# Nyström attention feeding a mixture of experts: batch 0's hidden layer split by token half, one pseudo-inverse chain for batches 2 and 3, and a new order

## The chip, the cores and the metric

The kernel runs on one core of one Trainium2 chip. The metric is the device time of one execution in microseconds. Three runs of the kernel before took 195.12, 196.12 and 197.24 us; the median is 196.12 us. The execution that was profiled took 197.17 us, and its trace spans 194.8 us from the first to the last instruction.

## The reference

There are 4 batches of 8 heads, 576 tokens and 64 dimensions. Attention is approximated with 32 landmarks, means of 18 tokens each:

```python
A  = sm(q, k_lm);  Bm = sm(q_lm, k_lm);  C = sm(q_lm, k)      # sm: scaled scores, softmax
Z  = Bm.T / (norm1(Bm) * norminf(Bm) + 1e-6)
for _ in range(6):
    Z = 2 * Z - Z @ Bm @ Z
x  = A @ Z @ C @ v
```

The 4 x 576 rows of `x` (512 wide) then go through a layer of 8 experts. Each row goes to the expert with the largest logit `x @ w_gate`; `h = relu(x @ w1[e])` has 1024 columns, `y = h @ w2[e]` 512, and the output row is `y` times the gate's probability. An expert takes 576 rows at most; later rows give zeros.

## The kernel before

**Work.** For these inputs all rows of a batch choose one expert, and only three batches get one, so the kernel guesses one expert per batch, computes batches 0 to 2 with it and writes zeros for batch 3. At the end a count, `nrest`, tells every engine whether the guess fails; a branch then leads either to a general version or to an `Else` that holds only the last step (`finish`, L1012 to L1015: half an output tile is scaled on VectorE and stored).

**Per batch.** `loads` brings q, k and v in on SyncE's queue. `landmarks` (L341) sums 18 tokens per landmark in four pieces of two head pairs, each on VectorE (V), on GpSimd as a tree of five adds (G), or on TensorE (P), by the string `lm`. `chain` (L435) is the softmax of q and k landmarks and six steps of the inverse, each a group of 16 small matmuls (`pp`, L512) and an add on VectorE (`PQ`, L517), up to `Wd` (L521). `cpath`, `cjoin` and `cval` make C times v. `apath(b, 0)` and `apath(b, 1)` make A for the first and the second half of the tokens: transpose, maximum, subtraction, exponential, sum, reciprocal, product, transpose to `AT` (L668). `mpart` and `gate` join these to `MT` and to the gate's matrix; `logits` and `probs` follow. `guess` and `pick` (L390) find the expert's number `ei` of batch 0 early, from the values alone; for the later batches it comes from `Gg`.

**Per expert batch.** `w1load` brings four chunks of w1 (512 KB each, three buffers, so the fourth waits until the first was used) and `wload` eight of w2. `gstage` (L883) folds `MT` into w1: one or two chunks at a time in one PSUM buffer `sc`, then a rounded copy `gh` (ScalarE, L903) and the rest `gl` (VectorE, L905), two buffers each. `ffn` (L910) then runs 8 chunks `fc` of 128 hidden columns times 2 token halves `c`, in that nesting: six matmuls (L945, "a piece" below), a relu into `hx`, and the relu's remainder on VectorE (L970) or GpSimd (L968). The output tiles follow (L1003, and L1008 for the 64 rows that are left over). `hx` exists once, so the hidden layer of the next batch starts after the outputs of the one before.

**Order.** The instructions' order is not written by hand. Each function above yields steps with an engine, an estimated cost, dependences and a priority; `weave` (L90) simulates the engines in order and always emits the step that could start first, or among those that could start nearly as early the one with the lowest priority number. The priorities (`pr`, `fr`, `sp`, `ah`, `rl`, `ev`) and the engine strings stand in `CFG`. Every engine runs its instructions in the order in which they were emitted, and all loads and nearly all stores share SyncE's queue. Where the simulated TensorE would be idle before the first output tile, `fill` (L1063) puts matmuls on zeros into a bank that nobody reads.

Of the kernel before, what the change touches and what calls it, by code (L numbers as in the profile page):

```python
# [9 lines left out]
F32 = mybir.dt.float32  # L10
# [8 lines left out]
class Step:  # L19
    def __init__(self, eng, cost, deps=(), order=(), name=None, res=None, nres=1, keep=False, free=None, prev=True, start=0, prio=None,  # L20
# [9 lines left out]
    sc='AAAA',  # L30
    rx='GGVVGVVVGVGGVGVGVGVVVGGGVVGVGGVGVGGVVVVVGVGGVVGG',
    look=0.05,
    tg='fftftftffftftffftffttfff',
    ce='AVAVAAAA',
    pa='sfssfffs',
    aw='GVGGGGGVGVGVGGGG',
    ye='VVVAAVVVAVVVAAVV',
    lm='VVVVGPVGGVGGVVGV',
    al='GVGGGV',
    lo='GGVVGGGGGVGVVVVVVGGGVVGG',  # L40
    pr=[
# [4 lines left out]
    ],  # L46
    fr=[
        [2750, 908, 1024, 2472, 1325, -961],
        [1075, 1146, 4950, 3350, 855, -3473],
        [1756, -242, 588, 4127, 1063, 1667],  # L50
    ],
    sp=[-3688, 3402, -434],
    ah=[-4252, -3823, 2101],
    rl=[-7657, -3393, -1471],
    ev=[-2134, 1163, 1326],
# [10 lines left out]
spawned = []  # L66
# [117 lines left out]
def nystrom_moe(ctx: ExitStack, tc: tile.TileContext, q, k, v, vtail, wgate, w1, w2, out, cap):  # L184
# [92 lines left out]
    PQs = [[keep.tile([128, NG, 3, 32], F32, name=f"PQ{i}{y}") for y in range(2)] for i in range(2)]  # L277
    for t in (*PQs[0], *PQs[1]):
        nc.gpsimd.memset(t[:, :, 1, :], 0.0)
    BBs = [keep.tile([128, 4, 2, 32], F32, name=f"BB{i}") for i in range(2)]  # L280
    for t in BBs:
        nc.vector.memset(t[:, 0:2, 1, :], 1e-9)
        nc.vector.tensor_copy(t[:, 2:4, 1, :], istk.unsqueeze(1).to_broadcast([128, 2, 32]))
# [6 lines left out]
    cse = [keep.tile([128, NG, 2], F32, name=f"ce{i}") for i in range(2)]  # L290
# [50 lines left out]
    def landmarks(b):  # L341
        lmt[b] = dict(q=None, k=None)
        for g in range(2):
            for nm in "qk":
# [9 lines left out]
                if e == "V":  # L354
                    parts = ((2, 3), (3, 4)) if b == 0 and g and nm == "k" else ((2 * g, 2 * g + 2),)
                    for i, (j0, j1) in enumerate(parts):
                        last = i + 1 == len(parts)
                        yield Step("V", 60 + 600 * (j1 - j0), deps=[f"ld{b}{nm}{j}" for j in range(j0, j1)], order=order,
                                   prev=False, name=f"lm{b}{g}{nm}" if last else None)
                        nc.vector.tensor_reduce(out=lm()[:, j0:j1, :], axis=AX.X, op=ALU.add,  # L360
                                                in_=st[b][nm][:, j0:j1, :].rearrange("p y (m t) -> p y m t", t=L))
# [12 lines left out]
                else:  # L374
                    yield Step("G", 1300, deps=ld, order=order + ([f"lmg{b - 1}"] if b else []), prev=False)
                    tr = sm.tile([128, 2 * M, 9], F32, tag="tr", name="tr", bufs=1)
                    x = st[b][nm][:, 2 * g:2 * g + 2, :].rearrange("p y (m t) -> p (y m) t", t=L)
                    nc.gpsimd.tensor_tensor(tr, x[:, :, 0:9], x[:, :, 9:18], ALU.add)
                    yield Step("G", 725)
                    nc.gpsimd.tensor_tensor(tr[:, :, 0:4], tr[:, :, 0:4], tr[:, :, 4:8], ALU.add)  # L380
                    yield Step("G", 460)
                    nc.gpsimd.tensor_tensor(tr[:, :, 0:2], tr[:, :, 0:2], tr[:, :, 2:4], ALU.add)
                    yield Step("G", 380)
                    nc.gpsimd.tensor_tensor(tr[:, :, 0:1], tr[:, :, 0:1], tr[:, :, 8:9], ALU.add)
                    yield Step("G", 330, name=f"lm{b}{g}{nm}")
                    nc.gpsimd.tensor_tensor(lm()[:, 2 * g:2 * g + 2, :].rearrange("p y m -> p (y m)").unsqueeze(2),
# [43 lines left out]
    gr = [128, NG, 32]  # L430
# [4 lines left out]
    def chain(b):  # L435
        PA = PQs[b % 2]
        p = Step("P", 222, tag="a", deps=LM(b), order=[f"wd{b - 2}", f"mt{b - 2}"] if b > 1 else (), name=f"bp{b}", res="sc", keep=True)
        yield p
        bp = psc.tile([128, 2, 512], F32, tag="sc", name="bp")[:, :, 0:32]
        for j in range(4):  # L440
            for x in range(NG):
                y = slice(64 * x, 64 * x + 64)
                nc.tensor.matmul(bp[32 * j:32 * j + 32, x, :], lhsT=lmt[b]["q"][y, j], rhs=lmt[b]["k"][y, j],
                                 start=True, stop=True)
        yield V(110)
        bst = sm.tile([128, 2, NG], F32, tag="bst", name="bst")
        BB = BBs[b % 2]
        Bst = BB[:, 0:2, 0]
        BT = BB[:, 2:4]
        nc.vector.tensor_reduce(out=bst[:, 0, :], in_=bp, axis=AX.X, op=ALU.max)  # L450
        yield V(125, free=p)
        nc.vector.tensor_tensor(Bst, bp, bst[:, 0, :].unsqueeze(2).to_broadcast(gr), ALU.subtract)
        yield Step("A", 150)
        nc.scalar.activation(Bst, Bst, AF.Exp, scale=SC2)
        yield V(130)
        nc.vector.tensor_reduce(out=bst[:, 1, :], in_=BB[:, 0:2].rearrange("p x a m -> p x (a m)")[:, :, 0:33], axis=AX.X,
                                op=ALU.add)
        yield V(80)
        nc.vector.reciprocal(bst[:, 1, :], bst[:, 1, :])
        if CFG["sc"][b] == "V":  # L460
            yield V(133, port=True)
            nc.vector.tensor_tensor(Bst, Bst, bst[:, 1, :].unsqueeze(2).to_broadcast(gr), ALU.mult)
        else:
            yield Step("A", 420)
            for x in range(NG):
                nc.scalar.activation(Bst[:, x], Bst[:, x], AF.Copy, scale=bst[:, 1, x:x + 1])
        yield V(162)
        nc.vector.transpose(BT[:, :, 0], Bst)
        rc = sm.tile([128, 4], F32, tag="rc", name="rc")
        cc = sm.tile([128, 2, NG], F32, tag="cc", name="cc")  # L470

        def norms():
            yield V(190)
            nc.vector.tensor_reduce(out=rc, in_=BB[:, :, 0], axis=AX.X, op=ALU.add)
            yield V(225)
            rct = sm.tile([128, 4, 32], F32, tag="rct", name="rct", bufs=1)
            nc.vector.transpose(rct, rc.unsqueeze(2).to_broadcast([128, 4, 32]))
            yield V(190)
            nrm = sm.tile([128, 2, NG], F32, tag="nrm", name="nrm")
            nc.vector.tensor_reduce(out=nrm.rearrange("p a g -> p (a g)"), in_=rct, axis=AX.X, op=ALU.max)  # L480
            yield V(230)
            for x in range(NG):
                nc.vector.tensor_scalar(cc[:, 0, x:x + 1], nrm[:, 0, x:x + 1], nrm[:, 1, x:x + 1], 1e-6, op0=ALU.mult,
                                        op1=ALU.add)
            yield V(80, name=f"cc{b}")
            nc.vector.reciprocal(cc[:, 1, :], cc[:, 0, :])

        spawned.append(norms())
        p = Step("P", 356, res="ch", keep=True)
        yield p  # L490
        bbp = pch.tile([128, NG, 2, 32], F32, tag="ch", name="bbp")
        for x in range(NG):
# [3 lines left out]
        yield V(380, free=p, deps=[f"cc{b}"])  # L496
        PQ = PA[0]
        for x in range(NG):
            nc.vector.scalar_tensor_tensor(PQ[:, x, 0:3:2], bbp[:, x], cc[:, 1, x:x + 1], i0, ALU.mult, ALU.subtract, reverse1=True)
        for it in range(6):  # L500
            last = it == 5
            p = Step("P", 417 if last else 356, res="ch", keep=True)
            yield p
            pp = pch.tile([128, NG, 2, 32], F32, tag="ch", name="pp")
            for x in range(NG):
# [9 lines left out]
            yield V(200, free=p)  # L515
            Pn = PA[1 - it % 2]
            nc.vector.tensor_tensor(Pn[:, :, 0:3:2, :], pp, PQ[:, :, 1:3, :], ALU.add)  # L517
            PQ = Pn
        yield V(340, free=p, name=f"wd{b}")
        Wd = sm.tile(n4, F32, tag="Wd", name="Wd")  # L520
# [619 lines left out]
```

## Time and profile before

| | us |
|---|---|
| median of three runs | 196.12 (195.12 to 197.24) |
| profiled execution | 197.17 |
| its span | 194.8 |
| TensorE busy | 182.0 (93%) |
| VectorE busy | 114.7 (59%) |
| ScalarE busy | 79.0 (41%) |
| GpSimd busy | 77.8 (40%) |

The granted clock of TensorE was 0.989 of full speed over the span. The busy time of TensorE counts the matmuls on zeros as well. In the chain of work that ended last TensorE holds 67% of the span, VectorE 18%. The hidden layers of the three batches start at 34.87, 100.07 and 146.88 us, and the last matmul starts at 187.83 us.

### The profile page before, as it was taken

Reading aid. Unit: us, or ns where it says so; the run is one execution under the profiler, and the core shown is the slowest. Engines: PE = TensorE matmul, PEld = TensorE weight load, DVE = VectorE, ACT = ScalarE, POOL = GpSimd, SP = SyncE. Lnnn points to the kernel's source line nnn. Section 1 sums busy time; section 2 is a strip of 40 time slices with the busy share of each in tenths; the row PEclk is TensorE's granted clock in tenths of the full one; section 3 lists DMA queues with packets and bytes.
Section 4 is the critical chain, followed back from the end, with each engine's and each line's share of the span. In section 5 each row is a group of like instructions: output and inputs, shape, how many; then the busy total and the mean of one; then the engine's idle time right before and its main releaser. Section 6 shows DMA issues by size and latency. Waiting matters only on the chain.

```text
span 194.8 us, 5551 instructions
## 1 busy us (share of the span) xinstructions
PE 182.0 (93%) x2212; PEld 138.7 (71%) x2219; DVE 114.7 (59%) x349; ACT 79.0 (41%) x200; POOL 77.8 (40%) x127
## 2 busy tenths in 40 slices
PE   7999979998999998999999999999999989999960
PEld 2446854785966686766797897688888887888950
DVE  3699996877659999985398657580015451210010
ACT  3023615873853441341768476500067664101100
POOL 7219378795896282400051357200054744000000
PEclk9999999999999999999999999999999999999995
DMA  5999839983304968956244009811137000111111
GB/s 202 386 410 385 327 107 354 374 310 98 122 0 135 382 247 245 321 195 195 108 140 133 0 21 326 307 29 54 54 109 220 0 0 2 32 54 56 56 35 34
DMA packets 17492, 31.95 MB, mean 164 GB/s; under 512 B 1520, under 2 KB 9584, under 8 KB 17456
## 3 DMA queue, kind: packets, MB, share of 16 engines
q1 hardware_dynamic: 17024, 31.07, 45.5%
q8 instruction: 19, 0.31, 0.7%
q10 hardware_dynamic: 432, 0.43, 0.6%
q14 instruction: 17, 0.14, 0.2%
HBM read 26.77 MB, written 4.72 MB: 162 GB/s over the span
## 4 chain that ended last, share of the span: by engine, by line
PE 67%; DVE 18%; ACT 4%; issue 4%; DMA 3%; SPq 2%; DVEq 0%
PE hps L945 16%; PE yps L1003 16%; PE ybank L1003 12%; PE ybank L1066 5%; PE ybank L1008 5%; DMA w2t<-in_w 3%; PE gps L673 2%; PE psA L640 2%; PE pp L512 2%; DVE AT L668 1%; SPq L854 1%; DVE amx L660 1%; PE cvp L611 1%; DVE lmk L360 1%; DVE AW L665 1%
## 5 line engine op out<-in xcount | busy, mean ns | idle before, releaser
L1003 PE MATMUL yps<-wh,hx 128*128 128x512 f32 (+1 forms) x112 | 34.4, 378 | 0.0
L968 POOL TENSOR_TENSOR hx<-rr,hx 128x224 fp32r<-128x224 f32 (+2 forms) x35 | 21.4, 631 | 25.1 <-ACT hx L959 25.0
L879 POOL TENSOR_TENSOR wl<-w2t,wh 128x512 fp32r<-128x512 f32 x13 | 17.0, 1321 | 34.1 <-ACT wh L873 34.0
L945 PE MATMUL hps<-ah,gh 128*128 128x288 f32 x96 | 29.7, 309 | 0.9 <-ACT rr L957 0.7
L945 PE MATMUL hps<-ah,gl 128*128 128x288 f32 x96 | 28.4, 296 | 0.5 <-DVE gl L905 0.5
L1003 PE MATMUL ybank<-wh,hx 128*128 128x512 f32 (+1 forms) x96 | 28.9, 374 | 0.0
L945 PE MATMUL hps<-al,gh 128*128 128x288 f32 x96 | 28.3, 295 | 0.0
L1003 PEld LDWEIGHTS yps<-wh,hx 128*128 128x128 f32 x112 | 20.6, 188 | 4.0 <-issue 0.2
L1003 PE MATMUL yps<-wl,hx 128*128 128x512 f32 (+1 forms) x56 | 21.0, 374 | 0.0
L945 PEld LDWEIGHTS hps<-ah,gh 128*128 128x128 f32 x96 | 18.0, 188 | 3.4 <-ACT rr L957 0.9
L1003 PEld LDWEIGHTS ybank<-wh,hx 128*128 128x128 f32 x96 | 17.6, 188 | 3.1
L945 PEld LDWEIGHTS hps<-ah,gl 128*128 128x128 f32 x96 | 18.0, 188 | 0.7 <-DVE gl L905 0.7
L945 PEld LDWEIGHTS hps<-al,gh 128*128 128x128 f32 x96 | 18.0, 188 | 0.1
L1003 PE MATMUL ybank<-wl,hx 128*128 128x512 f32 (+1 forms) x48 | 17.8, 372 | 0.0
L551 ACT ACTIVATE Cx<-psC,cs 128x320 f32<-128x320 f32 (+1 forms) x16 | 7.9, 499 | 22.0 <-DVE cs L546 22.0
L970 DVE SCALAR_TENSOR_TENSOR hx<-hps,hx 128x288 fp32r<-128x288 f32 (+2 forms) x37 | 12.0, 353 | 8.1 <-ACT hx L962 7.9
L873 ACT CAST wh<-w2t 128x512 fp32r<-128x512 f32 x24 | 14.6, 625 | 2.2 <-DMA w2t<-in_w 2.0
L879 DVE TENSOR_TENSOR wl<-w2t,wh 128x512 fp32r<-128x512 f32 x11 | 9.0, 848 | 9.4 <-ACT wh L873 9.4
L1066 PE MATMUL ybank<-wt 128*128 128x512 bf16 x43 | 13.0, 446 | 1.6 <-DVE wt L216 1.3
L1029 DVE TENSOR_SCALAR yo<-yps,fac 128x512 f32<-128x512 f32 (+1 forms) x4 | 2.7, 681 | 17.1 <-PE yps L1003 17.1
L905 DVE TENSOR_TENSOR gl<-gps,gh 128x512 fp32r<-128x512 f32 x12 | 8.1, 684 | 7.8 <-ACT gh L903 7.8
L1003 PEld LDWEIGHTS yps<-wl,hx 128*128 128x128 f32 x56 | 10.6, 189 | 1.8
(193 smaller groups left out, 340.5 us busy)
## 6 DMA issues: line engine op xcount, KB each, us to landing
w1t<-in_w SPq DMA_DIRECT2D x12, 512.0 KB, 6.1
w2t<-in_w SPq DMA_DIRECT2D x24, 256.0 KB, 3.2
qt<-in_q SPq DMA_DIRECT2D x8, 576.0 KB, 6.6
vm<-in_v SPq DMA_DIRECT2D x8, 512.0 KB, 8.0
kt<-in_k SPq DMA_DIRECT2D x7, 576.0 KB, 7.4
out<-yo SPq DMA_DIRECT2D x10, 256.0 KB, 2.1
out<-wt SPq DMA_DIRECT2D x4, 256.0 KB, 7.1
kt<-in_k SPq DMA_DIRECT2D x2, 288.0 KB, 7.2
```

Source lines behind the costliest of these rows:

```text
L512: nc.tensor.matmul(pp[y, x], lhsT=PQ[y, x, 0], rhs=PQ[y, x, 0:3:2], start=True, stop=True)
L551: nc.scalar.activation(Cx[:, x, :], t[:, x, :n], AF.Exp, bias=cs[:, 1, x, a:a + 1], scale=SC1, accum_out=sums[:, x, a:a + 1])
L640: nc.tensor.matmul(ps[x][32 * j:32 * j + 32, :HS], lhsT=lmt[b]["k"][y, j], rhs=st[b]["q"][y, j, HS * a:HS * a + HS], start=True, stop=True)
L873: nc.scalar.copy(wh, w2t)
L879: (nc.gpsimd if e == "G" else nc.vector).tensor_tensor(wl, w2t, wh.bitcast(F32), ALU.subtract)
L905: nc.vector.tensor_tensor(gl, ps, gh.bitcast(F32), ALU.subtract)
L945: nc.tensor.matmul(ps[:, :HS], lhsT=wt[:, g, fs], rhs=a[:, g, ss], start=(n == 0), stop=(n == 3 * NG - 1))
L968: nc.gpsimd.tensor_tensor(dst, rr[:, x0 - s0:x1 - s0], hi, ALU.subtract)
L970: nc.vector.scalar_tensor_tensor(dst, ps[:, x0 - s0:x1 - s0], 0.0, hi, ALU.max, ALU.subtract)
L1003: nc.tensor.matmul(ps[:, :dn], lhsT=hx[:, fc, o:o + 128], rhs=wt[:, d0:d1], start=(fc == 0 and o == t0 and wt is wh), stop=(fc == NFC - 1 ...
L1008: nc.tensor.matmul(ps[:m], lhsT=hx[:, fc, t0:t0 + m], rhs=wt, start=(fc == 0 and wt is wh), stop=(fc == NFC - 1 and wt is wh))
L1066: nc.tensor.matmul(ybank, lhsT=wt[:, 0:128], rhs=wt, start=True, stop=True)
```

## The change

Batch 0's hidden layer does all eight chunks of the first token half, then the second half in the order 4 to 7, 0 to 3. So that all four chunks of `gh` and `gl` exist at once, chunks 2 and 3 are kept in the part of `hx` that the second half will overwrite. The chains of batches 2 and 3 become one, whose instructions work on both batches; it starts when the landmarks of both are there. `cjoin` needs fewer and wider VectorE instructions. The landmark string has a new letter H (batch 0's q piece of group 1): one head pair on VectorE, the other on GpSimd; batch 1's k piece of group 0 goes from TensorE to GpSimd, its k piece of group 1 from GpSimd to VectorE. The first of the two half-width output tiles at the end is scaled on ScalarE whatever `ye` says. All priorities and several engine strings are new, and so is the order that `weave` makes of them.

```diff
-    sc='AAAA',
-    lm='VVVVGPVGGVGGVVGV',
-    al='GVGGGV',
+    sc='AAAV',
+    lm='VVHVGGVVGVGGVVGV',
+    al='VGGVVV',
...
-        [-4438, 311, -2721, -3616, 1794, 1235, 314, -4333, -5239, 2994],
+        [-7286, -3191, -2420, -1936, -6900, 1466, -3803, -545, -5759, -2168],
...
+                    if e == "H":
+                        yield Step("V", 720, deps=ld[:1], order=order, prev=False, name=f"lv{b}{g}{nm}")
+                        nc.vector.tensor_reduce(out=lm()[:, j0, :], axis=AX.X, op=ALU.add,
+                                                in_=st[b][nm][:, j0, :].rearrange("p (m t) -> p m t", t=L))
+                        j0, n = j0 + 1, 1
...
-    def chain(b):
+    def chain(*bs):
+        two = len(bs) == 2
+        n = len(bs) * NG
...
+        p = Step("P", C(222, 352), tag="a", deps=[x for b in bs for x in LM(b)],
...
-            p = Step("P", 417 if last else 356, res="ch", keep=True)
+            p = Step("P", C(417, 770) if last else C(356, 672), res="ch", keep=True)
             yield p
-            pp = pch.tile([128, NG, 2, 32], F32, tag="ch", name="pp")
-            for x in range(NG):
+            pp = pch.tile([128, n, 2, 32], F32, tag="ch", name="pp")
+            for x in range(n):
...
-        yield V(260)
-        for x in range(NG):
-            t = cm[:, 1, x:x + 1]
-            nc.vector.tensor_scalar(t, sums[:, x, 0:1], cf[:, 0, x, 0:1], 1e-9, op0=ALU.mult, op1=ALU.add)
-            nc.vector.scalar_tensor_tensor(t, sums[:, x, 1:2], cf[:, 0, x, 1:2], t, ALU.mult, ALU.add)
+        yield V(70, port=True)
+        nc.vector.tensor_tensor(sums[:, :, 0:2], sums[:, :, 0:2], cf[:, 0], ALU.mult)
+        yield V(80)
+        nc.vector.tensor_reduce(out=cm[:, 1], in_=sums, axis=AX.X, op=ALU.add)
         yield V(80)
         nc.vector.reciprocal(cm[:, 1], cm[:, 1])
-        yield V(260, name=f"cg{b}")
-        for x in range(NG):
-            for i in range(2):
-                nc.vector.tensor_scalar(cf[:, 1, x, i:i + 1], cf[:, 0, x, i:i + 1], cm[:, 1, x:x + 1], None, op0=ALU.mult)
+        yield V(80, port=True, name=f"cg{b}")
+        nc.vector.tensor_tensor(cf[:, 1], cf[:, 0], cm[:, 1].unsqueeze(2).to_broadcast([128, NG, 2]), ALU.mult)
...
+                if key == 0 and c >= 2:
+                    hx = hidden(b)
+                    gh, gl = (hx[:, y:y + 2, HS:HS + FH].rearrange("p i (g f) -> p g i f", g=NG) for y in (2 * c, 2 * c - 4))
...
-        for fc in range(NFC):
-            fs = slice(128 * (fc % 2), 128 * (fc % 2) + 128)
-            for c in range(2):
+        late = [(fc + 4) % NFC for fc in range(NFC)] if key == 0 else list(range(NFC))
+        pieces = [(fc, 0) for fc in range(NFC)] + [(fc, 1) for fc in late] if key == 0 else [(fc, c) for fc in range(NFC) for c in range(2)]
+        for fc, c in pieces:
...
-                e = CFG["ye"][k] if full else "A"
+                e = CFG["ye"][k] if dn == DM and full else "A"
...
-        parts = [loads(b), landmarks(b), chain(b), route(b), cpath(b, 0), cpath(b, 1), apath(b, 0), apath(b, 1), cjoin(b), cval(b)]
+        parts = [loads(b), landmarks(b), chain(*([b] if b < 2 else [2, 3])) if b < 3 else iter(()), route(b), cpath(b, 0), cpath(b, 1), apath(b, 0), apath(b, 1), cjoin(b), cval(b)]
```

## Rows read from the trace of the kernel before

**Rows 1.** Busy time by stretch: length, then PE, PEld, DVE, ACT, POOL, clock, DMA.

```profile
10.00:35.00 25.00, 23.15 (x476) 15.06 (x482) 22.52 (x70) 9.98 (x32) 15.79 (x20) 1.00 0.86 318
35.00:50.00 15.00, 14.07 (x254) 11.22 (x255) 12.02 (x46) 10.66 (x29) 10.97 (x17) 1.00 0.66 234
```

**Rows 2.** Groups by line and shape on TensorE: busy us, mean ns.

```profile
L1066 PE MATMUL ybank<-wt 128*128 128x512 bf16 x43 | 13.0, 446 | 1.6 <-DVE wt L216 1.3 <-issue 0.2
...
L371 PE MATMUL lmp<-kt,ident 128*128 128x64 f32 x36 | 4.9, 302 | 0.1
```

**Rows 3.** The chain of work that ended last: start us, us, what.

```profile
1.30 8.82 PE ybank L1066 x29
...
49.70 4.98 PE hps L945 x36
...
185.33 0.50 DVE yo L1029
...
186.05 3.04 issue
189.35 0.48 DVE yo L1014
```

**Rows 4.** Timeline, 20 to 47 us, several engines: start us, us, engine, line.

```profile
20.06 0.22 DVE L396 SCALAR_TENSOR_TENSOR sel<-glg,gm,rev 128x8 f32<-128x8 f32 x1
...
24.59 0.14 DVE L398 TENSOR_REDUCE fxs<-sel 128x1 f32<-128x8 f32 x1
...
26.35 2.87 SPq L854 DMA_DIRECT2D w1t<-in_w  x3
...
30.06 0.42 DVE L521 TENSOR_TENSOR Wd<-pp,bmask 128x256 f32<-128x256 f32 x1 [0.56 <-PE pp L510]
...
32.14 0.66 PE L673 MATMUL gps<-w1t,MT 64*32 64x256 f32 x16
...
34.38 0.39 SPq L854 DMA_DIRECT2D w1t<-in_w  x1
...
34.87 0.40 PE L945 MATMUL hps<-ah,gh 128*128 128x288 f32 x1
...
43.23 1.09 PE L673 MATMUL gps<-w1t,MT 64*32 64x256 f32 x32
...
45.14 0.40 PE L945 MATMUL hps<-ah,gh 128*128 128x288 f32 x1
```

**Rows 5.** VectorE by line and shape, 10 to 30.5 us: busy us, mean ns.

```profile
L668 DVE STREAM_TRANSPOSE AT<-AW 128x576 f32<-128x576 f32 x2 | 1.5, 770 | 0.0
...
L360 DVE TENSOR_REDUCE lmk<-kt 128x32 f32<-128x576 f32 x2 | 1.4, 744 | 0.0
L360 DVE TENSOR_REDUCE lmq<-qt 128x64 f32<-128x1152 f32 x1 | 1.3, 1329 | 0.0
...
L649 DVE STREAM_TRANSPOSE AW<-psA 128x576 f32<-128x576 f32 x1 | 0.8, 785 | 0.1
L665 DVE TENSOR_TENSOR AW<-AW,amx 128x576 f32<-128x576 f32 x1 | 0.7, 749 | 0.0
...
L599 DVE TENSOR_SCALAR cf<-cf,cm 128x1 f32<-128x1 f32 x4 | 0.6, 207 | 0.0
```

**Rows 6.** DMA issues between 34 and 35 us: line, KB each, us to landing.

```profile
w1t<-in_w SPq DMA_DIRECT2D x1, 512.0 KB, 7.1
```

**Rows 7.** Timeline, 71 to 74 us, GpSimd and VectorE.

```profile
71.42 1.44 POOL L923 TENSOR_TENSOR al<-AT,ah 128x576 fp32r<-128x576 f32 x1
...
71.55 1.92 DVE L665 TENSOR_TENSOR AW<-AW,amx 128x576 f32<-128x576 f32 x1
```

**Rows 8.** Timeline of TensorE: output matmuls behind a chain step, and the last matmul.

```profile
91.03 0.50 PE L1003 MATMUL yps<-wh,hx 128*128 128x512 f32 x1
91.36 0.39 PE L1003 MATMUL yps<-wl,hx 128*128 128x512 f32 x1
...
187.83 0.28 PE L1003 MATMUL ybank<-wh,hx 128*128 128x256 f32 x1
```

More of the change, by code (lines that the diff above doesn't have):

```diff
@@ L289, in nystrom_moe @@
         nc.gpsimd.memset(t[:, :, 32:33], 1e-9)
-    cse = [keep.tile([128, NG, 2], F32, name=f"ce{i}") for i in range(2)]
+    cse = [keep.tile([128, NG, 3], F32, name=f"ce{i}") for i in range(2)]
+    for t in cse:
+        nc.vector.memset(t[:, :, 2:3], 1e-9)
     CT1 = keep.tile([128, NG, 3, 128], F32, name="CT1")
@@ L357, in landmarks @@
                         last = i + 1 == len(parts)
-                        yield Step("V", 60 + 600 * (j1 - j0), deps=[f"ld{b}{nm}{j}" for j in range(j0, j1)], order=order,
+                        yield Step("V", 720 if j1 - j0 == 1 else 1290, deps=[f"ld{b}{nm}{j}" for j in range(j0, j1)], order=order,
                                    prev=False, name=f"lm{b}{g}{nm}" if last else None)
@@ L429, in nystrom_moe, with C @@
     n4 = [128, NG, 4, 32]
-    gr = [128, NG, 32]
     def V(c, **kw):
         return Step("V", c, **kw)
-    def chain(b):
-        PA = PQs[b % 2]
-        p = Step("P", 222, tag="a", deps=LM(b), order=[f"wd{b - 2}", f"mt{b - 2}"] if b > 1 else (), name=f"bp{b}", res="sc", keep=True)
-        yield p
-        bp = psc.tile([128, 2, 512], F32, tag="sc", name="bp")[:, :, 0:32]
-        for j in range(4):
-            for x in range(NG):
[L442 to L453, printed above, removed]
+    def chain(*bs):
+        two = len(bs) == 2
+        n = len(bs) * NG
+        b0 = 0 if two else NG * (bs[0] % 2)
+        xs = slice(b0, b0 + n)
+        grn = [128, n, 32]
+        sfx = "2" if two else ""
+        bufs = 1 if two else 2
+        def C(one, both):
+            return both if two else one
+        p = Step("P", C(222, 352), tag="a", deps=[x for b in bs for x in LM(b)],
+                 order=[f"{w}{b - 2}" for b in bs if b > 1 for w in ("wd", "mt")], name=[f"bp{b}" for b in bs], res="sc", keep=True)
+        yield p
+        bp = psc.tile([128, 2, 512], F32, tag="sc", name="bp")
+        for i, b in enumerate(bs):
+            for j in range(4):
+                for x in range(NG):
+                    y = slice(64 * x, 64 * x + 64)
+                    nc.tensor.matmul(bp[32 * j:32 * j + 32, x, 32 * i:32 * i + 32], lhsT=lmt[b]["q"][y, j], rhs=lmt[b]["k"][y, j],
+                                     start=True, stop=True)
+        bp = bp[:, :, 0:32 * len(bs)].rearrange("p x (i m) -> p i x m", m=32)
+        yield V(C(110, 175))
+        bst = sm.tile([128, 2, len(bs), NG], F32, tag="bst" + sfx, name="bst", bufs=bufs)
+        bsf = bst.rearrange("p a i x -> p a (i x)")
+        Bst = BBs[:, 0, xs, 0]
+        BT = BBs[:, 1, xs]
+        nc.vector.tensor_reduce(out=bst[:, 0], in_=bp, axis=AX.X, op=ALU.max)
+        yield V(C(125, 190), free=p)
+        nc.vector.tensor_tensor(Bst.rearrange("p (i x) m -> p i x m", x=NG), bp,
+                                bst[:, 0].unsqueeze(3).to_broadcast([128, len(bs), NG, 32]), ALU.subtract)
+        yield Step("A", C(150, 205))
@@ L493, in chain @@
+        for x in range(n):
             for j in range(4):
@@ L495, in chain @@
                 nc.tensor.matmul(bbp[y, x], lhsT=BT[y, x, 0], rhs=BT[y, x], start=True, stop=True)
[L496 to L498 removed]
+        yield V(C(380, 760), free=p, deps=[f"cc{bs[0]}"])
+        PQ = PQs[0][:, xs]
+        for x in range(n):
             nc.vector.scalar_tensor_tensor(PQ[:, x, 0:3:2], bbp[:, x], cc[:, 1, x:x + 1], i0, ALU.mult, ALU.subtract, reverse1=True)
@@ L881, in wsplit, with hidden @@
             later(lo, e, 1280 if e == "G" else 610, name=f"ws{key}{c}", port=True)
+    def hidden(b):
+        if "hx" not in st[b]:
+            st[b]["hx"] = ff.tile([128, NFC, 2 * S], F32R, tag="hx", name="hx")
+        return st[b]["hx"]
     def gstage(b, key):
+        st[b].pop("hx", None)
         MT = MTk[b]
@@ L983, in ffn @@
             ps = None
-            for fc0 in range(0, NFC, 2):
-                last = fc0 + 2 == NFC
+            seq = late if n == 0 else list(range(NFC))
+            for fc0 in seq[::2]:
+                last = fc0 == seq[-2]
                 s = Step("P", (1360 if dn == DM else 715) if full else 919, prev=False, kind="Y",
```

231 lines of the change are left out of this document (115 added, 116 removed), and 6 rows, old and new, of the table pr.

## The prediction

> **What bounds the kernel now.** I read the busy times by stretch first. Between 10 and 35 us TensorE is busy 23.15 of 25 us and VectorE 22.52; between 35 and 50 us they are at 14.07 and 12.02 of 15 [rows 1]. That looks like a TensorE bound from end to end, but part of it isn't work: of 43 matmuls on zeros [rows 2], 29 lie ahead of 10.1 us [rows 3], so 14 fall behind it. At 8.82 / 29 = 0.30 us each [rows 3] they are 4.2 us at most. Another 4.9 us are a landmark sum that TensorE makes because it is free [rows 2]. So the stretch from 10 to 35 us holds about 23.2 - 4.2 - 4.9 = 14.0 us of matmuls that the rest needs, and 11.0 us are the ceiling of what a better beginning can give. There VectorE is the bound: it is 90% busy, and what TensorE waits for passes through it.
>
> The timeline shows the wait. `sel`, the input of the guessed expert's number, exists at 20.28 us, and the next step `fxs` starts at 24.59, 4.3 us later, with VectorE busy on other things. The loads of w1 follow at 26.35 us, `Wd` of batch 0 starts at 30.06, the first product of w1 at 32.14, the first piece of the hidden layer at 34.87 [rows 4]. Weights and `MT` thus arrive nearly together, and both come off VectorE's queue late.
>
> From 34.87 us on TensorE is close to full. It loses 0.93 us between 35 and 50 us [rows 1] and little later. At the very end the chain leaves TensorE: VectorE scales the first half tile at 185.33 us, then jumps to the other branch, which takes 3.04 us, and scales the second half at 189.35 [rows 3]. TensorE's last matmul started at 187.83 and lasted 0.28 [rows 8], so its result waited more than a microsecond for VectorE's jump.
>
> **The change part by part.** The sum is made against the profiled execution, 197.17 us, which is 1.05 us above the median of the runs.
>
> *The end.* The first half tile goes to ScalarE. VectorE's last work ahead of the branch is then an earlier tile, and its jump of 3.04 us [rows 3] lies beside the last matmuls. The second half tile can start when TensorE is done, at 188.11 us, plus about 0.1 to see it: 188.2 instead of 189.35. That is **-1.1 us**. More isn't there, since TensorE then bounds; less, down to 0, if another engine arrives last: ScalarE takes over the 0.5 us scaling and its store, and jumps after them, but nothing of the second half waits for ScalarE.
>
> *The front.* With the first half of the tokens ahead, the hidden layer can start without A's second half. Six VectorE instructions, from a transpose of 0.79 to one of 0.77 us [rows 5], about 4.0 us together, may move behind `Wd`. The landmark that is shared with GpSimd takes 0.74 instead of 1.33 on VectorE [rows 5]: 0.6 less. In `cjoin` eight one-column instructions become two products and a sum. Four of the eight hold VectorE for 0.6 us [rows 5], so all for 1.2; at 0.14 for a small sum, as `fxs` shows [rows 4], and an estimated 0.2 for each product, the size of a one-column one [rows 5], the new three take 0.5: 0.7 less. Against that stands one more landmark piece of batch 1 on VectorE, 1.33 [rows 5]. So VectorE loses 4.0 us of work ahead of `Wd` if that piece comes early, and 5.3 if it comes late. In a queue that is 90% full nearly all of it should show, both in `Wd` and in the expert's number, whose 4.3 us of waiting is VectorE's queue alone. The steps that lie on ScalarE and TensorE stay. I take 3.5 us, near the 4.0; the bounds are 0 (the new order spends the time on batch 1) and 5.3.
>
> Not all of that reaches the end. The 14.0 us of needed matmuls had 25 us, and a shorter front has room for them but not always the inputs; what isn't ready moves behind and costs its own length. I take 1.0 us back, between 0 and the whole 3.5. The landmark that leaves TensorE costs nothing there and saves nothing by itself, since matmuls on zeros stand beside it; on GpSimd, idle for 9.2 of those 25 us [rows 1], it hides as long as batch 1 isn't urgent. The front is **-2.5 us**.
>
> GpSimd's added work has a price where both engines meet: a VectorE product that began 0.13 us behind a GpSimd subtraction took 1.92 us [rows 7], where the same instruction took 0.75 in the first stretch [rows 5]. So such a meeting costs about 1.2 us. The Trainium skill ("SBUF — State Buffer", section "Who interferes with whom") says that a VectorE instruction with two SBUF inputs and a GpSimd one that reads SBUF exclude each other for a whole instruction; the row agrees, and by that rule GpSimd's extra adds would cost the front two meetings, for A's product and for the rest of A's copy, and the sum would be 2.4 us worse.
>
> *The order of the pieces.* This is where the change can hurt. The fourth chunk of w1 is issued at 34.38 us, behind the first product of 32.14 [rows 4], and lands 7.1 us later [rows 6], at 41.5. From the start of a product to the first piece that uses it go 34.87 - 32.14 = 2.7 us [rows 4]. So chunk 4's first piece can't start before 44.2 us, 9.3 us behind the first piece. A piece takes 6 x 4.98 / 36 = 0.83 us [rows 3], and the four pieces of the first half that are ready last 3.3 us, while before seven pieces could run until 45.14, with the product of 43.23 between them [rows 4]. So three pieces, 2.5 us, have to be replaced by other work: A's second half and batch 1's scores, which the new order leaves for just this place. The lower bound is -0.9 (no hole, and the old idle time gone), the upper 2.5. I take a hole of 1.6 where 0.9 was idle: **+0.7 us**.
>
> *The shared chain.* Seven groups of 16 matmuls of batch 2 ride with those of batch 3. Their columns stay; what goes is the break in the output matmuls. The first output matmul behind a chain step shows 0.50 us where the next has 0.39 [rows 8]; with as much on the way in, a break costs 0.2, and seven cost 1.4 where each stands alone. Many stand beside other short groups, so I take **-0.6 us**, between 0 and -1.4. That batch 2's chain now waits for batch 3's landmarks costs nothing: its hidden layer starts at 146.88 us, and output matmuls cover the time until then. VectorE's saved instructions there, and the engine strings, I cost at nothing, since TensorE covers them; a new stall could cost what 35 to 50 us has, 0.9.
>
> The sum is -1.1 - 2.5 + 0.7 - 0.6 = **-3.5 us**: 193.7 for the profiled execution, and 192.6 against the median of 196.12.
>
> **The rivals.** *The front's gain is eaten.* The change doesn't do what it could: the order puts batch 1's landmarks or A's second half ahead of the guess all the same, or the meetings with GpSimd take the gain, and the first piece still starts near 34 us. Then -1.1 + 0.7 - 0.6 = -1.0 is left: 195.1 us. For it speaks that the priorities are new as a whole and that VectorE stays the fullest engine there; against it, that six instructions no longer have to be early.
>
> *All of it shows.* The front gives 5.3 and nothing back, and there is no new hole, because the loads of w1 come early too: -1.1 - 5.3 - 0.6 = -7.0, or 189.1 us. The ceiling of 11.0 allows it; the 14.0 us of needed matmuls, which would have less time, speak against it.
>
> *The hole decides* (slower). If the front doesn't move and nothing else is ready when the four pieces are done, TensorE stands still from 38.2 to 44.2 us. That is 6.0 us, and with -1.1 and -0.6 the time is +4.3, 200.4 us. It makes the kernel slower by over 1% from a hole of 3.7 us on. The fixed distance of 9.3 us speaks for it; against it, that before TensorE had some 3.5 us of other work in that stretch (10.3 us between the first and the eighth piece, less seven pieces of 0.83 and 0.93 idle), and gets A's second half besides.
>
> **How the numbers follow.** A measurement of this kernel can tell about 1% from no change, so 194.2 and 198.1 us are the limits. The forecast gets 0.50; its own range is 190.0 (nothing given back and no hole, the old idle time gone: 2.6 us below it) to 194.4 (the hole at its bound: 1.8 above). The eaten front gets 0.22, all of it showing 0.13, the hole 0.15. Faster is then the forecast but for its upper edge, all of it showing, and a little of the first rival: 0.64. Slower is the hole, 0.14; the same 0.22. The range takes in 189.1 at the low end and half of the hole's cases at the high end: 188.8 to 197.8.
>
> **What would show it.** In the trace after, `fxs` and the loads of w1 should start 3 us or more earlier, and the first piece near 31.4 us. Between the fourth and the fifth piece of the first half there should be short groups, not idle time over 2 us. The last half tile should start within 0.2 us of the last matmul's end, with no jump between. There should be one set of chain groups with 32 matmuls. I am wrong if the first piece stays behind 34 us, if chunk 4 of w1 leaves TensorE idle for 4 us, or if VectorE's queue lets the output tiles run dry between 50 and 100 us.

## The result, and the profile after

The changed kernel takes 188.19 us (median of 4 runs, 187.60 to 189.38), the kernel before 195.62 beside it (195.00 to 197.24): a ratio of 0.961, with a 95% interval of 0.955 to 0.967. In a second comparison it took 188.69 us, 0.962 [0.957, 0.967]. That is 7.4 us less, twice my 3.5, and the time lies just below my range. Executions that took over 1.5% longer than the fastest of their kernel are left out of all medians below.

The profiled execution took 188.28 us, 8.89 less than that of before. The chain of waits gives the first split. Its end after the change, start and length in us:

```profile
180.11 2.89 PE ybank L1031 x24
...
183.18 0.48 DVE yo L1042
```

The second half tile starts 0.2 us behind TensorE's last matmul, and the jump of 3.04 us [rows 3] is gone from the chain. TensorE ends at 182.98 us instead of 188.11: 5.13 us. From there to the end of the span it is 3.61 us instead of 6.67. Of these 3.06 us 1.06 are the jump; 2.0 are one slow landing of the last store, 3.9 us instead of 1.7, in the one execution of before that stood in the prediction (it is not there in a second one, below). The last 0.70 lie outside the spans.

So 5.1 us have to be found ahead of TensorE's end. Busy time of TensorE from 35 us and from 50 us to its end: length, busy (matmuls), clock, DMA share, GB/s. Before:

```profile
35.00:188.11 153.11, 150.10 (x1709) 1.00 0.40 136
50.00:188.11 138.11, 136.03 (x1457) 1.00 0.37 126
```

After:

```profile
35.00:182.98 147.98, 146.89 (x1693) 1.00 0.40 134
50.00:182.98 132.98, 132.73 (x1370) 1.00 0.37 125
```

Behind 35 us TensorE was idle for 153.11 - 150.10 = 3.01 us, now 1.09: 1.92 gone. It is busy for 150.10 - 146.89 = 3.21 us less. The two make the 5.13. And of the 3.01 us idle, 138.11 - 136.03 = 2.08 lay behind 50 us, where I had "little"; now 0.25 do. The second executions of both kernels (below) show 2.04 and 0.21.

The waits of TensorE behind 35 us (us, times, longest) name them. Before:

```profile
PE hps L945 <- ACT rr L957: 0.7, 1, 0.7
PE ltp L728 <- DVE AT L668: 0.5, 1, 0.5
PE pp L512 <- DVE PQ L517: 0.5, 1, 0.5
PE hps L945 <- DVE gl L905: 0.5, 1, 0.5
PE pp L512 <- issue: 0.4, 1, 0.4
PE bp L443 <- DVE cm L595: 0.3, 1, 0.3
PE hps L945 <- DVE hx L970: 0.2, 1, 0.2
```

After:

```profile
PE pp L531 <- DVE PQ L536: 0.5, 1, 0.5
PE gps L691 <- ACT Cx L572: 0.3, 1, 0.3
```

Seven waits, each of a kind that came once, became two. Five of the seven were for a result of VectorE, one for ScalarE, none for a transfer.

The same view for one tile at a time says where the busy time went. The chain's tiles `pp` (x336) and `bbp` (x48), before:

```profile
35.00:200.00 165.00, 8.14 (x336) 0.98 0.38 127
...
35.00:200.00 165.00, 1.28 (x48) 0.98 0.38 127
```

After:

```profile
35.00:200.00 165.00, 6.71 (x336) 0.99 0.36 121
...
35.00:200.00 165.00, 1.07 (x48) 0.99 0.36 121
```

As many matmuls, 1.64 us less. One group shows why: "90.74 0.36 PE pp L512 x16" in the chain of before, "92.45 0.58 PE pp L531 x32" after, so twice the matmuls cost 0.58 instead of 0.72. For the rest, `psA` falls from 3.03 to 1.92 us (64 matmuls to 48: one group of 16 now lies ahead of the first piece), and `bp` from 0.82 to 0.59. The outputs `yps` and `ybank` fall from 80.89 to 79.46 for the same 360 matmuls, and the pieces `hps` rise from 42.21 to 43.42. Short groups break the outputs into 11 stretches before and 5 after, the pieces into 12 and 19: they moved from the outputs to the pieces.

The stretches that answer to [rows 1] and the zeros that answer to [rows 2]:

```profile
10.00:35.00 25.00, 22.13 (x468) 11.98 (x463) 23.48 (x69) 10.70 (x33) 18.43 (x26) 1.00 0.95 357
35.00:50.00 15.00, 14.16 (x325) 10.61 (x325) 13.94 (x45) 9.60 (x26) 7.86 (x11) 1.00 0.70 218
```

```profile
L1094 PE MATMUL ybank<-wt 128*128 128x512 bf16 x58 | 15.7, 407 | 1.8 <-DVE wt L216 1.3 <-issue 0.5
```

Of the 58 matmuls on zeros 26 lie behind 10 us and take 7.3 us, where before 15 took 4.3. VectorE is fuller than before from 10 to 35 us, 23.48 against 22.52, and between 25 and 30 us it is full:

```profile
25.00:30.00 5.00, 3.67 (x89) 1.58 (x89) 5.00 (x11) 0.95 (x4) 3.52 (x6) 1.00 0.98 322
```

The timeline of after shows what that means for the front (start us, us, engine, line); it answers to [rows 4]:

```profile
21.00 0.14 DVE L405 TENSOR_REDUCE fxs<-sel 128x1 f32<-128x8 f32 x1
...
22.52 0.27 DVE L536 TENSOR_TENSOR PQ<-pp,PQ 128x128 f32<-128x128 f32 x1
23.48 1.73 SPq L872 DMA_DIRECT2D w1t<-in_w  x3
23.61 0.28 DVE L536 TENSOR_TENSOR PQ<-pp,PQ 128x128 f32<-128x128 f32 x1
23.81 1.34 DVE L361 TENSOR_REDUCE lmq<-qt 128x64 f32<-128x1152 f32 x1
25.07 0.28 DVE L536 TENSOR_TENSOR PQ<-pp,PQ 128x128 f32<-128x128 f32 x1
...
27.62 1.29 POOL L385 TENSOR_TENSOR tr<-qt 128x576 f32<-128x576 f32 x1
...
27.85 1.08 DVE L567 TENSOR_SCALAR cs<-cs 128x2 f32<-128x2 f32 x1
...
28.22 0.25 PE L529 MATMUL pp<-PQ,istk 32*32 32x32 f32 x7
...
28.85 0.76 DVE L678 TENSOR_REDUCE amx<-AW 128x18 f32<-128x594 f32 x1
29.53 0.41 DVE L541 TENSOR_TENSOR Wd<-pp,bmask 128x256 f32<-128x256 f32 x1
...
29.99 0.44 PE L700 MATMUL mtp<-Wd,CV 128*64 128x128 f32 x4 [0.77 <-DVE Wd L541]
30.03 1.29 DVE L361 TENSOR_REDUCE lmk<-kt 128x64 f32<-128x1152 f32 x1
31.37 0.27 DVE L703 COPY MT<-mtp 128x128 f32<-128x128 f32 x1
...
34.69 0.40 PE L972 MATMUL hps<-ah,gh 128*128 128x288 f32 x1
```

The guess came 3.6 us earlier (`fxs` at 21.00), the loads of w1 2.9, and the first piece 0.18. What it waits for is `MT`, and `MT` did not move (31.14 before, 31.37 after). The steps from `PQ` to `Wd` and `MT` of batch 0's chain are round trips between VectorE and TensorE, and VectorE does other work between them. The last `pp` products end at 28.47 us and `Wd` starts at 29.53, behind `cs` and `amx`; `mtp` ends at 30.43 and the copy to `MT` starts at 31.37, behind a landmark. From the first `PQ` to `MT` such waits of finished products for VectorE add up to 4.0 us after, and to 2.5 us before. Before, TensorE kept the chain waiting as well:

```profile
22.29 0.23 DVE L517 TENSOR_TENSOR PQ<-pp,PQ 128x128 f32<-128x128 f32 x1
22.45 1.60 PE L371 MATMUL lmp<-kt,ident 128*128 128x64 f32 x12
23.98 0.43 PE L512 MATMUL pp<-PQ 32*32 32x64 f32 x16
```

That is a landmark on TensorE, which the change moved to GpSimd: 1.46 us from the end of `PQ` to the next products, where it is 0.06 at the same place after. The chain lost about as much waiting for TensorE as it gained waiting for VectorE.

Between the end of the fourth piece of the first half and the start of the fifth (40.0 and 43.62 us) there were short groups, as hoped; the idle time from 35 to 50 us is 15 - 14.16 = 0.84 us, against 0.93 before (0.64 and 0.45 in the second executions).

### The profile page after: what moved, and what is told of

Read it like the earlier page. It is cut to its first block, busy times and chain, and to the rows that moved or that the text cites. A ratio compares the mean times of both kernels' runs of the same rounds, so it can differ in the third digit from the quotient of the medians.

```text
span 186.6 us, 5484 instructions
## 1 busy us (share of the span) xinstructions
PE 177.7 (95%) x2191; PEld 136.0 (73%) x2199; DVE 108.2 (58%) x313; ACT 79.7 (43%) x202; POOL 78.6 (42%) x131
## 4 chain that ended last, share of the span: by engine, by line
PE 71%; DVE 14%; DMA 6%; ACT 3%; issue 3%; POOL 2%; SPq 0%; DVEq 0%; ACTq 0%
PE yps L1031 19%; PE hps L972 17%; PE ybank L1031 16%; PE ybank L1036 6%; DMA qt<-in_q 3%; PE gps L691 3%; DMA w2t<-in_w 2%; PE pp L531 2%; DVE cs L565 2%; PE ctp L582 1%; PE cvp L629 1%; PE psC L559 1%; DVE gl L933 1%; PE psA L658 1%; ACT Cx L572 1%
## 5 line engine op out<-in xcount | busy, mean ns | idle before, releaser
L972 PE MATMUL hps<-ah,gh 128*128 128x288 f32 x80 | 25.2, 315 | 0.1
L972 PE MATMUL hps<-al,gh 128*128 128x288 f32 x80 | 23.6, 295 | 0.0
L972 PE MATMUL hps<-ah,gl 128*128 128x288 f32 x80 | 23.6, 295 | 0.0
L1055 ACT ACTIVATE yo<-yps,fac 128x512 f32<-128x512 f32 (+1 forms) x5 | 3.2, 647 | 32.5 <-PE yps L1031 32.5
L972 PEld LDWEIGHTS hps<-ah,gh 128*128 128x128 f32 x80 | 15.0, 188 | 2.8 <-ACT BB L486 0.4
L972 PEld LDWEIGHTS hps<-al,gh 128*128 128x128 f32 x80 | 15.1, 188 | 0.0
L972 PEld LDWEIGHTS hps<-ah,gl 128*128 128x128 f32 x80 | 15.0, 188 | 0.0
L572 ACT ACTIVATE Cx<-psC,cs 128x256 f32<-128x256 f32 (+1 forms) x16 | 8.0, 499 | 15.6 <-DVE cs L567 15.4
L984 ACT ACTIVATE rr<-hps 128x288 f32<-128x288 f32 x23 | 9.5, 411 | 6.8 <-PE hps L972 6.6
L1094 PEld LDWEIGHTS <-wt 128*128 128x128 bf16 x65 | 6.1, 104 | 8.3 <-issue 2.8
```

What stands on the lines that cost most here:

```text
L572: nc.scalar.activation(Cx[:, x, :], t[:, x, :n], AF.Exp, bias=cs[:, 1, x, a:a + 1], scale=SC1, accum_out=sums[:, x, a:a + 1])
L972: nc.tensor.matmul(ps[:, :HS], lhsT=wt[:, g, fc % 2], rhs=a[:, g, ss], start=(n == 0), stop=(n == 3 * NG - 1))
L984: nc.scalar.activation(rr, ps[:, :HS], AF.Relu)
L1094: nc.tensor.matmul(ybank, lhsT=wt[:, 0:128], rhs=wt, start=True, stop=True)
```

## The experiments

In five groups: the end, the parts with the new order kept, each structure with an order of its own, the front, the end once more.

**The kernel before once more**, unchanged.

> The kernel before, unchanged, for a second profile. In its first profile the last store (issued at 189.87 us) held the end until 193.77 us, 3.9 us, where the changed kernel's last store (183.69) was in by 185.6 us, 1.9 us. Theory A: those 2.0 us belong to that one execution (it took 197.17 us where others took 195.0 and 195.1), so here the last store lands in about 2 us and the span is near 193 us. Rival: they belong to how the kernel before ends, so 3.9 us again and a span near 194.8 us.

194.98 us in the profiled execution, and TensorE ends at 188.09 us as in the first (188.11), but the span ends 4.68 us later instead of 6.67. The last store landed in 1.7 us instead of 3.9: the 2.0 us belong to the one execution.

**The end alone, in the kernel before:** the first half tile on ScalarE.

```
-    ye='VVVAAVVVAVVVAAVV',
+    ye='VVVAAVVVAVVVAAAV',
```

> The kernel before with one letter changed: the first half-width tile at the end is scaled on ScalarE. Nothing else in any engine's order changes. Theory A: VectorE's jump leaves the end of the chain, the last half tile starts within 0.2 us of TensorE's end: -1.2 us (ratio 0.994). Rival 1: the late VectorE also delays the last store, so -3 us (ratio 0.984). Rival 2: another engine arrives last, 0.

193.61 us, ratio 0.994 [0.990, 0.998] to 194.57. The chain ends with

```profile
184.30 2.89 PE ybank L1003 x24
...
187.37 0.48 DVE yo L1014
```

and the distance from TensorE's end to the span's end fell from 4.68 to 3.63 us. The end is worth 1.05 us.

**Parts undone, the new priorities kept.** First the chains of batches 2 and 3 apart, then the pieces of batch 0 nested as before (with that nesting's order tags and split as well).

```
-  chain(*([b] if b < 2 else [2, 3])) if b < 3 else iter(())
+  chain(b)
```

> The changed kernel with one chain for batch 2 and one for batch 3 again, all priorities as they are, so the rest of the order shifts with it. Theory A: the shared chain is worth the 1.2 us by which its groups are shorter on TensorE (32 small matmuls in 0.58 us against twice 0.36) and some breaks, so +1.2 to +2.5 us against the changed kernel, 189.5 to 190.7 us. Rival: it is worth 4 us or more because it also frees VectorE between 50 and 77 us, 192 us or more. Rival 2: nothing, 188.2 us.

```
-  pieces = [(fc, 0) for fc in range(NFC)] + [(fc, 1) for fc in late] if key == 0 else [...]
+  pieces = [(fc, c) for fc in range(NFC) for c in range(2)]
...
```

> The changed kernel with batch 0's pieces in the old nesting (both halves of a chunk, then the next chunk), all priorities as they are. Theory A: the first piece did not come earlier by the new order, so the order itself is worth little: within 1 us of 188.2 us if A's second half still arrives in time, with the first piece near 34.7 us. Rival: the order is what lets VectorE do batch 1's landmarks early; the first piece then starts 2 to 4 us later than 34.7 us, and the time is 190 to 192 us.

215.73 us (1.107 [1.102, 1.112]) and 207.29 (1.064 [1.060, 1.069]), far outside of what any theory gave. They do not price the parts. Two stretches of the two-chain kernel (columns as in [rows 1]), and a piece of its chain of waits:

```profile
90.00:100.00 10.00, 6.85 (x186) 3.40 (x174) 7.42 (x18) 3.28 (x6) 4.73 (x4) 0.83 0.72 250
100.00:110.00 10.00, 2.35 (x21) 1.80 (x22) 8.56 (x17) 1.48 (x3) 6.76 (x8) 0.67 1.05 378
```

```profile
95.97 7.01 DMA qt<-in_q
...
103.05 1.30 POOL tr L385
```

A load of q, issued behind other work, landed at 102.98 us, and GpSimd's landmark sums and TensorE's work waited for it: 7.65 us of idle TensorE in ten. So these two times price the mismatch of a structure with an order drawn up for another.

**Each structure with priorities and engine strings of its own**, all drawn up by the same means; the code as in the parts above, the tables replaced (here the first row of the first):

```
     pr=[
-        [-7286, -3191, -2420, -1936, -6900, 1466, -3803, -545, -5759, -2168],
+        ...
```

> The kernel after, with batches 2 and 3 in chains of their own, and with priorities and engine strings drawn up anew for that structure (the 215.7 us of the same structure under the changed kernel's order were an order made for something else). Theory S (the shared chain is worth what its merged groups save, 14 groups instead of 7, with at most 0.2 us a break and 0.15 us a pair of groups): 189.5 to 191 us, a ratio of 0.970 to 0.978. Theory O (the new order alone is worth the gain, the structure nothing): 188 to 188.7 us. Theory D (the two structures carry the gain, no order gets it without them): 193 us or more.

> The kernel after, with the pieces of batch 0 nested as before (both halves of a chunk together), and with priorities and engine strings drawn up anew for that. The first piece did not move in the changed kernel, so the split of batch 0 by halves should be worth little: theory S and theory O both expect 188 to 189.5 us (ratio 0.961 to 0.97), with the first piece near 34.5 us or a little later. Theory D expects 193 us or more, with TensorE idle or on other groups ahead of 37 us.

> The kernel before, its code as it was, with priorities and engine strings drawn up anew for it by the same means and for as long as for the other structures. Theory O (the new order carries the gain): 188 to 190 us, a ratio of 0.96 to 0.97; the idle time of 2.96 us between the first piece and TensorE's last matmul falls to about 1. Theory D (the structures carry it): 194 to 196 us, a ratio of 0.99 to 1.00, as the order was tuned already. Theory S lies between: 191 to 192.5 us, since the end's 1.1 us and the chain's 1 to 2 stay behind.

> The kernel after, its code as it is, with priorities and engine strings drawn up anew by the same means: the control. If a fresh order by itself moved the time, it would show here. All theories expect 187 to 190 us (ratio 0.956 to 0.97); a time outside that range says how far an order that the same means finds can miss, and by so much the three others are uncertain.

> Batches 2 and 3 in chains of their own, in a second new order. Theory D (the shared chain is worth 4 us or more of time, by TensorE's shorter groups and fewer waits): 194 us or more, as the first order's 196.9. Theory O (the 6.3 us between two chains and the control were the luck of an order): 189 to 193 us. In either case the TensorE time without matmuls on zeros and without idle time is about 165.0 us, against 162 to 163 of the shared chain.

> Batch 0's pieces nested as before, the chain shared, in a second new order. Theory D: 193 us or more, as the first order's 194.2. Theory O: 188 to 192 us, no worse than the control's 190.6 by more than an order's luck of 2.4 us.

> The code before in a second new order. Theory D: 194 us or more, for the third time for this code. Theory O: at least one order in three comes out near 190 us.

> The code after in a second new order, the second control. Theory D: 192 us or less, as 188.4 and 190.6. Theory O: anywhere between 188 and 196 us; a time of 194 us or more would take the ground from the reading that the structures carry the gain.

Time in us for each order, and TensorE's busy time for `pp` and `bbp` together over the whole span of the two new ones:

```
code                        given order    new     second new   pp + bbp
before                      195.6          197.8   201.2        12.4, 13.1
two chains, halves split    215.7 (after's) 196.7  193.2        12.4, 12.7
shared chain, nested        207.3 (after's) 194.1  194.2        11.3, 11.3
after                       188.2          190.6   203.1        10.8, 11.5
```

After the first column of new orders the theory that the structures carry the gain looked good: the code before took 7.2 us more than the control (the kernel after in a new order). The second column took it down, by the condition that was set for it: the control took 203.1 us (1.040 [1.029, 1.051]), the two chains 193.15 (0.985 [0.977, 0.993]). An order's luck on this kernel is some 15 us, more than any part that could be priced. That the order alone carries the gain isn't shown either: three orders of the code before gave no median under 194.6.

Only the last column ranks the codes whatever their order. A shared chain takes 10.8 to 11.5 us of TensorE, separate ones 12.4 to 13.1. The kernels before and after stand at 12.46 and 10.83, and the two-chain kernel under the priorities of after, where nothing else in the code differs, at 12.17. So the shared chain is worth 0.7 to 2.2 us of TensorE's busy time, and it is the one part that was shown by itself, besides the end. What it is worth in the kernel's time no run shows.

**The front.** The kernel after with batch 0's split landmark whole on VectorE:

```
-    lm='VVHVGGVVGVGGVVGV',
+    lm='VVVVGGVVGVGGVVGV',
```

> The kernel after as it is, beside the other three, so that they are read against it and not only against the kernel before. A ratio of 0.961 (0.955 to 0.967), TensorE's last matmul within 0.5 us of 183.0 us and 26 matmuls on zeros behind 10 us, as in its first profile. A time above 189.5 us would say that the size of the gain is not repeatable.

> The kernel after with batch 0's split landmark whole on VectorE (1.33 us there instead of 0.74, five additions fewer on GpSimd), the priorities as they are. Theory Q (VectorE's queue bounds the beginning, as the prediction had it): the guess, Wd and the first piece come 0.6 us later, and the time rises by 0.3 to 0.6 us. Theory L (the beginning is a chain of dependent steps, and VectorE's other work fits between them: a landmark of 1.34 us between two steps of the chain lengthened it by 0.37): the first piece moves by less than 0.25 us unless the landmark itself is on the chain, and the time by less than 0.3 us.

The kernel after took 188.69 us this time, and with the landmark on VectorE 188.59 (0.962 [0.957, 0.967]). The first piece starts at 34.58 us, against 34.41 and 34.69 in the two profiles of the kernel after. 0.6 us of VectorE are worth nothing measurable here, as theory L expected. But they did not reach the stretch where VectorE is full. In the kernel after, VectorE stood idle ahead of the first `cs` until a TensorE group was done that had waited for GpSimd's part of that landmark; with the landmark whole on VectorE the same `cs` starts at 10.78 us without a pause. The kernel after:

```profile
11.46 0.69 DVE L565 TENSOR_REDUCE cs<-psC 128x2 f32<-128x512 f32 x1 [0.91 <-PE psC L559]
```

So the run does not decide between the theories for the time behind 20 us.

Then the beginning cleared, with new priorities:

```
-  deps=[f"ld{b}{nm}{j}" for j in range(j0, j1)], order=order,
+  deps=[f"ld{b}{nm}{j}" for j in range(j0, j1)], order=order + ["mt0"] * (b > 0),
...
-  yield V(670)
+  yield V(670, order=["wd0"] * (b == 0 and a == 1))
```

> The kernel after with the beginning cleared: batch 1's and 2's landmarks on VectorE wait for batch 0's MT, and the sum of A's second half waits for Wd; priorities and engine strings drawn up anew for that, as in the control with a new order. The steps of the chain should come every 1.0 to 1.1 us instead of up to 1.9, Wd near 28 us instead of 29.5, MT near 29 instead of 31.4; then the loads of w1 (issued near 23.5, landing 7.1 us later) are next, and the first piece starts near 33.4 us, 1.3 us earlier. Theory F (an earlier first piece shows at the end, as my forecast reckoned): 1 us or more below the control, 189.5 us or less. Theory G (the work that is put off is given back behind the first piece): the control's 190.6 us or more, with more idle time or fewer matmuls on zeros replaced between 35 and 100 us.

195.1 us, 0.995 [0.990, 0.999]. That is far from theory F's 189.5 and on the side of theory G (190.6 us or more, with more idle time), but the order is new here too, and an order's luck is larger than the distance. Its timeline:

```profile
20.72 0.29 DVE L536 TENSOR_TENSOR PQ<-pp,PQ 128x128 f32<-128x128 f32 x1
...
29.41 0.29 DVE L703 COPY MT<-mtp 128x128 f32<-128x128 f32 x1
...
32.35 0.40 PE L972 MATMUL hps<-ah,gh 128*128 128x288 f32 x1
```

The first piece came at 32.35 us, 2.3 us earlier than in the kernel after, and TensorE ended 5.6 us later, at 188.55, with 4.7 us of waits behind 35 us. An earlier first piece alone is not an earlier end. The first piece came earlier than expected, but the chain's steps came every 1.2 to 1.8 us and not every 1.0 to 1.1, and the chain wasn't faster: from the first `PQ` to `MT` it took 29.41 - 20.72 = 8.69 us, against 8.85 in the kernel after (22.52 to 31.37) and 8.85 in the kernel before (22.29 to 31.14). It only began 1.8 us earlier. The equal lengths are chance and no floor: in the other new orders the same stretch took 8.07 to 10.94 us. Step by step, the round trips themselves take 4.4 to 4.5 us in all three kernels. The rest is waiting, for VectorE 2.5 us before, 4.0 after and 2.1 here, for TensorE 1.9, 0.4 and 2.1. VectorE was busy for 7.24, 8.81 and 7.49 us of these stretches, so the beginning was not as clear as meant: a product of 1.45 us stood between two steps.

**The end, undone in the kernel after.** A first try was to put the first half tile back on VectorE; it picked the tile by a loop variable that had moved on, so it moved the full tile ahead of it.

```
-  e = CFG["ye"][k] if dn == DM and full else "A"
+  e = "V" if key == B - 2 and n == len(tiles) - 2 else CFG["ye"][k] if dn == DM and full else "A"
```

> The kernel after with the first half tile of the end back on VectorE, nothing else changed. Theory A (VectorE's jump of 3.0 us behind its first half tile holds up the second): the second half tile starts about 1.2 us behind TensorE's last matmul instead of 0.2, and the time rises by 1.0 to 1.2 us over the kernel after. Rival (the end is set by the stores, as PE's end and the span's end lie 3.6 us apart in both): no more than 0.3 us.

188.86 us, as the kernel after beside it (188.69). VectorE's branch was then at 178.3 us and TensorE done at 183.41, so a jump of 3.06 us, as in the next run, was over about 2 us earlier (an estimate): a jump that lies beside matmuls cost nothing here. The second try moved the half tile:

```
-  e = CFG["ye"][k] if dn == DM and full else "A"
+  e = "V" if dn != DM else CFG["ye"][k] if full else "A"
```

> The kernel after with the first half tile of the end, this time that tile and no other, on VectorE. Theory A: VectorE's jump of 3.0 us then lies behind that half tile, the second half tile starts 1.0 to 1.3 us behind TensorE's last matmul instead of 0.2, and the time rises by about 1.1 us over the kernel after, to 189.5 us (ratio 0.967). Rival (the end is set by the last stores): less than 0.3 us.

189.3 us, 0.971 [0.963, 0.980], against 0.962 [0.957, 0.967] without the edit; the two intervals overlap, so the time alone does not show it. TensorE ends at 182.75 us as without it (182.98 and 182.60), and the chain of waits ends with

```profile
180.61 3.06 issue
...
183.84 0.48 DVE yo L1042
```

so the second half tile starts 1.09 us late: theory A, as in the kernel before.

## Why the prediction was right and wrong

*The end* (-1.1 us): right in place and size, 1.05 when done alone, 1.06 between the two profiles, about 1.1 when undone.

*The front* (-2.5 us) is the first step that failed. "So VectorE loses 4.0 us of work ahead of `Wd`", I reckoned. It lost 0.1: from the start of the span to `Wd` it was busy for 24.16 us before and for 24.06 after, and up to `MT` for 1.3 us more than before (24.58 and 25.90). Of the six instructions of A's second half the transposes, the maximum and the sum stayed ahead of `Wd`. The new order also put in two more landmarks, one of batch 1 ahead of `Wd` and one of batch 2 ahead of `MT`. So the rival of the eaten front had the mechanism, though the work came ahead of `MT` and not of the guess, and its condition came true, a first piece still near 34 us (34.69). The bound that I named holds: finished products on the way to `MT` waited about 4.0 us for a full VectorE. The guess did come 3.6 us earlier, but the first piece did not wait for it. A meeting with GpSimd fell on that way too, at the two columns of `cs` (1.08 us, 0.13 elsewhere), and not at the two instructions that I had named, which took 0.93 us (A's product) and 0.75 (the rest of A's copy). And the landmark that left TensorE, which I said "saves nothing by itself", had kept the chain waiting for 1.46 us before. What the front gave instead is a group of `psA`, 1.11 us, that now lies ahead of the first piece.

But that rival's time, 195.1, fell too, since it had my other terms. *The stalls behind 50 us* are the second step that failed, a term that I put at nothing: "From 34.87 us on TensorE is close to full", it said, losing 0.93 us up to 50 us "and little later". It lost 2.08 us later, 0.25 now: 1.83 us that I held for 0. The row was there to be read, one more stretch in the view of [rows 1]. I priced "a new stall" and no old one. That these waits are gone is what the traces show; which part of the change took them away stays open, as the orders differ by more.

*The shared chain* (-0.6, bounds 0 and -1.4) is the third: "Their columns stay; what goes is the break in the output matmuls." The group itself got cheaper, its 32 matmuls taking 0.58 us where two groups of 16 take 0.72, and with it `pp` and `bbp` lost 1.64 us and `bp` 0.23. My price of a break, 0.2, was near: six fewer stretches of the outputs go with 1.43 us, 0.24 each. But seven more stretches of the pieces go with 1.21, so of the breaks only 0.2 us are left.

*The order of the pieces* (+0.7): -0.1, and +0.2 between the second executions, so about nothing. The fourth chunk was issued at 33.91 us, and the first piece behind the product that folds it in came at 43.62, 8.9 us behind the first, as the fixed distance had it; short groups of the chain and of batch 1 filled the place. The rival of the hole needed that "nothing else is ready", and something was.

By these terms -1.06 - 1.11 (front) - 1.83 - 1.87 - 0.1 make -6.0, and `hps` (+1.21) and the outputs (-1.43) add -0.2. The second execution of before and that of after differ by 194.98 - 188.28 = 6.7, the medians by 7.4; the rest, 0.5 to 1.2 us, lies outside the spans and between executions, and was not taken apart. A part of my base was wrong as well: the profiled execution of before held 2.0 us of one slow store. That the kernel got faster, as I had forecast, is partly luck: the front gave less than I took, and the stalls that I had at nothing gave 1.83 us.

## What to carry to other kernels

Before an engine's saved time is counted for a result, ask what the new order will put in its place, since here landmarks of later batches took a part of it. Then follow that result's own steps and note at each one how long a finished input waited for which engine: two equal lengths can be sums of different waits. List a nearly full engine's idle time to its last instruction, stretch by stretch, since small waits of different causes can go together under a new order. And when a change brings a structure and an order at once, no part can be priced by undoing it under the other's order; a measure that depends little on the order, here one tile's busy time, can.

## What the runs showed of the hardware that was not expected

TensorE can stand still in the middle of a group of ready matmuls. In the kernel after with a second new order it did so twice, for 2.74 and 2.58 us, at the last step of a chain, both times between matmuls of the same group. The chain of waits:

```profile
45.58 0.05 PE pp L529 x5
45.63 2.74 issue
48.37 0.18 PE pp L529
```

In that pause, between 46 and 47 us, the DMA queue of the kind "instruction" moved one of the 19 loads of 16 KB that it makes in the whole span (mean size 0.31 MB / 19). The second pause had one too. The profile shows no other reason, but that such a load is the cause isn't shown: the other 17 loads came without such a pause, and seven pauses of 0.85 to 2.26 us in other orders held no load of this kind. The kernel after had no pause of TensorE of this sort over 0.2 us, so it is a part of an order's luck that no count of work shows.

A VectorE instruction of two columns (L567 above) took 1.08 us beside a GpSimd addition of 1.29, 1.10 in the second profile, where another instance took 0.13. The Trainium skill ("SBUF — State Buffer", section "Who interferes with whom") counts this kind among those that can take the port pair shared with GpSimd, besides those with two SBUF inputs. The rows agree: it ended at 28.93 us, the addition at 28.91 (27.62 + 1.29). I had looked for such a meeting at the large products only.

The granted clock fell with TensorE's pauses: in the two-chain kernel under the order of after it was 0.83 on the mean of ten microseconds in which TensorE was busy for 6.85, and 0.67 in the next ten, where it was busy for 2.35. Of the two levels, 1.2 and 2.4 GHz, that is the lower for some two thirds of the stretch. The kernels before and after stay at the upper one up to their last stretch.
